# Masked row maxima of the two-block score tiles: memset and maximum in PSUM, or one VectorE instruction with an added mask

## The chip, the cores and the metric

One of the eight cores of a Trainium2 chip runs the kernel. The metric is the device time of one execution in microseconds (us), lower is better. The kernel before took 358.55 us, the median of 3 runs (357.07 to 360.89).

## The reference

For 8 batches and 8 heads, with 576 positions and 64 numbers per head, block-causal attention (blocks of 64 positions) is computed, and its output goes through a soft mixture of 8 experts with 4 slots each.

```
scores = q @ k.T / sqrt(64);  scores[block_i < block_j] = -1e9
attn = exp(scores - rowmax) / (rowsum + 1e-9);  x = attn @ v      # x: 4608 x 512
logits = x @ phi                                                   # 4608 x 32
slot inputs = softmax over positions of logits, transposed, @ x
h = relu(slot_input[e] @ w1[e]);  slot_out = h @ w2[e]
out = softmax over slots of logits @ slot_out
```

All inputs and the output are f32.

## The kernel before

The work goes by head pairs: 8 batches of 4 pairs make 32 pairs, numbered m. The 576 query rows of a head are handled in tiles that take only the keys a row may see. Tile "7" holds the 128 rows of blocks 6 and 7 with 512 keys, tile "5" the 128 rows of blocks 4 and 5 with 384 keys; each exists once for each of the two heads ("70", "71", "50", "51"). Tile "8" holds block 8 of both heads with 576 keys, and the tiles "3", "2", "1", "0" hold one block of both heads, with 256 to 64 keys. Only tiles 7 and 5 need a mask: their first 64 rows (partitions 0 to 63) may not see the last 64 keys.

For each pair the steps are these.

- SyncE (SP) loads q, k and v into slots of one large SBUF tile, `arena`, two slots each; POOL scales k (L420).
- PE forms the scores in PSUM: tile 7 and tile 5 in `qk` (L456), the others in `qkb` (L477). `scores` gives the PSUM bank of each; the table `BK` sets the banks.
- DVE takes the negated row maxima in `rowmax` into the small tile `stat`. Tile 7: a memset of 64x64 to -1e30 in PSUM (L492), then a TENSOR_REDUCE over 512 columns (L494). Tile 5: one memset of 64x128 for both heads (L488), then one TENSOR_REDUCE over both heads (768 columns, two results). The other tiles have a TENSOR_REDUCE alone, also L494.
- ACT takes the exponential in `expo` (L504): it reads the scores from PSUM, adds the negated maximum as bias, writes f32 probabilities into `arena` and the row sums into `stat`. In the trace that is an ACTIVATE and an ACTIVATION_READ_ACCUMULATOR.
- POOL adds epsilon to the sums (`zeps`, L514), DVE takes reciprocals (`zinv`, L510), POOL scales the probabilities (`norm`, L521).
- PE transposes the probabilities (L541), DVE and ACT copy them out of PSUM (L388 and L386), PE multiplies them with v (`pv`, L573, and `pv8`, L583), and the result is copied into `xT`.

Once a batch, the logits (L601, L608), the running softmax over positions and the slot inputs (L710, L730, L739, L748, L753) are added. From about 307 us on, the expert matmuls (L958, L978) and the output (L929 to L949) follow; nothing of the change runs there.

The order on each engine is written by hand: every step is recorded with a time by `at`, from the table `TM` (`rm70`, `rm71` and `rm5` are the maxima, one entry for both heads of tile 5), and the steps are issued in the order of those times. Each engine runs its own steps strictly in that order and waits on semaphores for the others. Eight matmuls on a zero tile, `idle`, run at the start (`warm`, L427); the tables that would place more of them (`FILL`, `FILL0`) are empty.

Of the kernel before, what the change touches and what calls it, by code (L numbers as in the profile page):

```python
# [10 lines left out]
BF16 = mybir.dt.bfloat16  # L11
AF = mybir.ActivationFunctionType
ALU = mybir.AluOpType
AX = mybir.AxisListType
# [9 lines left out]
EPS = 1e-9  # L24
NEG = -1e30


NC = {"7": 512, "5": 384, "8": 576, "3": 256, "2": 192, "1": 128, "0": 64}
# [3 lines left out]
COL = {"70": 0, "71": 1, "8": 2, "3": 3, "2": 4, "1": 5, "0": 6, "50": 7, "51": 8}  # L32
# [218 lines left out]
def tile_attention_softmoe(  # L251
# [9 lines left out]
    nc = tc.nc  # L261
    const = ctx.enter_context(tc.tile_pool(name="const", bufs=1))
# [11 lines left out]
            s0 = 16 * qd + 4 * g  # L274
            nc.vector.tensor_reduce(out=own[r, qd:qd + 1], in_=stack[r, s0:s0 + 4], axis=AX.X, op=ALU.add)

    idle = const.tile([128, 128], BF16, name="idle")
    nc.vector.memset(idle, 0.0)
    c_all = const.tile([128, 2, NC2, NS], F32, name="c_all")

# [52 lines left out]
    with ExitStack() as c1:  # L333
        xp = c1.enter_context(tc.tile_pool(name="xp", bufs=1, side="right"))
# [4 lines left out]
        def bank(k, i=0, z=""):  # L339
            n = BK.get(k + z, BK.get(k))[i]  # L340
            return ps_all[:, 512 * n:512 * n + 512]

        def banks(k, lo, n, z=""):
            a, c = BK.get(k + z, BK.get(k))
            return ps_all.rearrange("p (n c) -> p n c", c=512)[:, a:c + 1:c - a, lo:lo + n]
# [11 lines left out]
        phi_sb = area("phi").rearrange("p (c s) -> p c s", s=NS)  # L357

        dt = xp.tile([128, 256], F32, name="dt")

        def pads(late):
            if late:
                nc.gpsimd.memset(c_all, 0.0)
                return
            for x, n in (("8_0", 640), ("8_1", 640), ("2_0", 256), ("2_1", 256), ("0_0", 128), ("0_1", 128)):
                nc.gpsimd.memset(area("p" + x)[:, NC[x[0]]:n], 0.0)
            for i in range(NV):
                nc.gpsimd.memset(area(f"v{i}").rearrange("p (j c d) -> p j c d", j=2, c=NQ)[64:128, :, 4, :], 0.0)
            nc.gpsimd.memset(dt[:, 128:192], 0.0)
# [4 lines left out]
        def late(m):  # L374
            return {NP * NB - 1: "y", NP * NB - 2: "w", NP * NB - 3: "x", **FIRST}.get(m, f".{m % NP}")
# [19 lines left out]
        probs, xTs, xps = {}, {}, {}  # L395
# [28 lines left out]
        def warm(i):  # L424
            if i == 0:
                xps["w"] = bank("pb")
            nc.tensor.matmul(  # L427
                xps["w"], lhsT=idle[:, 0:128], rhs=idle[:, 0:64].unsqueeze(1).broadcast_to([128, 8, 64]), start=True, stop=True
            )


        def fill(bank, n):
            for _ in range(n):
                nc.tensor.matmul(
                    bank, lhsT=idle[:, 0:128], rhs=idle[:, 0:64].unsqueeze(1).broadcast_to([128, bank.shape[-1] // 64, 64]),
                    start=True, stop=True,
                )


        def scores(x, m):  # L440
            z = late(m)
            if x == "8":
                return banks("B8", 0, 288, z)
            if x[0] == "5":
                return bank("C5", int(x[1]), z)[:, 0:384]
            if x[0] == "7":
                return bank("A" + x, 0, z)
            j, lo = {"3": ("B30", 0), "0": ("B30", 256), "2": ("B21", 0), "1": ("B21", 192)}[x]
            return bank(j, 0, z)[:, lo:lo + NC[x]]
# [32 lines left out]

        def rowmax(m, x):
            st, u = stat[m % 2], COL[x if x != "5" else "50"]
            if x == "5":
                todo = [(u, 2, banks("C5", 0, 384, late(m)))]
                for _, n, sc in todo:
                    nc.vector.memset(sc[0:64, :, 320:384], NEG)  # L488
            else:
                todo = [(u, 1, scores(x, m))]  # L490
                if x[0] == "7":
                    nc.vector.memset(todo[0][2][0:64, 448:512], NEG)  # L492
            for u, n, sc in todo:
                nc.vector.tensor_reduce(  # L494
                    out=st[:, 0, u:u + n], in_=sc, axis=AX.XY if x == "8" else AX.X, op=ALU.max, negate=True
                )

        def expo(m, x):
            st, u = stat[m % 2], COL[x]
            sc = scores(x, m)  # L500
            pr = prob(m, x)[:, 0:NC[x[0]]]
            if x == "8":
                pr = pr.rearrange("p (n c) -> p n c", n=2)
            nc.scalar.activation(  # L504
                out=pr, in_=sc, func=AF.Exp, bias=st[:, 0, u:u + 1], accum_out=st[:, 1, u:u + 1],
            )

        def zinv(m, i):
# [3 lines left out]
        def zeps(m, i):  # L512
            st, c = stat[m % 2], slice(*ZG[i])
            nc.gpsimd.tensor_scalar(  # L514
                out=st[:, 2, c], in0=st[:, 1, c], scalar1=EPS, scalar2=1.0, op0=ALU.add, op1=ALU.mult
            )

        def norm(m, x):
# [276 lines left out]
        for i in range(WARM):  # L795
            at(-50 + 0.01 * i, warm, i)
# [32 lines left out]
        for k in AREAS:  # L829

            m = NM - 2 if k in ("q0", "ks0", "v0") or k[0] == "p" and k[-2:] == "_0" else NM - 1
            pvs = ("pv", "pa")
            ends[k] = end(m, ("UA", "UB", "UC") if k[0] in "qk" else pvs if k[0] == "v" or k[:2] == "pt" else GROUPS)
        for i in XIN:
            m = max(m for m in range(NM) if m % NXT == i)
# [19 lines left out]
    with ExitStack() as c2:  # L855
        start = c2.enter_context(ExitStack())
# [194 lines left out]
```

## Time and profile before

| what | before |
|---|---|
| median of 3 runs | 358.55 us (357.07 to 360.89) |
| the profiled execution | 360.34 us |
| its span, first to last instruction | 358.6 us |
| mean granted clock of TensorE | 0.988 |
| PE busy | 339.2 us, 95% of the span |
| DVE busy | 279.4 us, 78% |
| ACT busy | 258.3 us, 72% |
| POOL busy | 205.8 us, 57% |

PE is TensorE's matmuls, DVE VectorE, ACT ScalarE, POOL GpSimd, SP SyncE. L494 is line 494 of the kernel. Busy time is that of instructions; an engine that waits for another is not busy. The names in a row read output <- inputs: `ps` is PSUM, `arena` the large SBUF tile, `stat` the maxima, sums and reciprocals.

### The profile page before, as it was taken

The page shows a single profiled execution, that of the slowest core. Times are in us where ns is not written, and L with a number is a line of the kernel's source. Part 1 is how long each engine was busy: PE and PEld are TensorE (multiplying, and loading weights), DVE is VectorE, ACT ScalarE, POOL GpSimd, SP SyncE. Part 2 cuts the span into 40 slices and gives each one's busy share as a digit, 9 for nine tenths or more (in the row PEclk, how much of TensorE's full clock was granted, in tenths as well). Part 3 has the DMA queues.
Part 4 walks back from the last instruction along what each step waited for, and adds up shares of the span by engine and source line. Part 5 has one row for each costly group of instructions (what it writes and reads, how often), then busy time and mean ns, then how long its engine had stood idle before and what let it go on. Part 6 is the DMA issues. An engine that isn't in the chain of part 4 may idle for free.

```text
span 358.6 us, 14247 instructions
## 1 busy us (share of the span) xinstructions
PE 339.2 (95%) x5664; PEld 233.7 (65%) x5664; DVE 279.4 (78%) x750; ACT 258.3 (72%) x855; POOL 205.8 (57%) x475
## 2 busy tenths in 40 slices
PE   8899999998999999989999999999999999999990
PEld 3567677765777677757676777677766786337660
DVE  5989888995799979977999789978998856563351
ACT  3987888784898789868978897889788884122241
POOL 4786848854767676666757585758574872100000
PEclk9999999998999999999999999999999999999997
DMA  5676455375236744482268343841441139999987
GB/s 165 195 274 223 139 187 181 103 264 202 69 114 204 254 144 144 151 308 78 79 210 277 85 173 104 318 150 58 132 124 60 37 98 421 430 424 423 409 335 318
DMA packets 28929, 72.27 MB, mean 202 GB/s; under 512 B 6848, under 2 KB 15168, under 8 KB 23872
## 3 DMA queue, kind: packets, MB, share of 16 engines
q1 hardware_dynamic: 28864, 71.38, 56.2%
q8 instruction: 44, 0.72, 0.8%
q14 instruction: 21, 0.17, 0.1%
HBM read 61.93 MB, written 9.44 MB: 199 GB/s over the span
## 4 chain that ended last, share of the span: by engine, by line
PE 69%; DVE 9%; ACT 7%; POOL 5%; DMA 4%; issue 2%; SPq 0%; DVEq 0%; ACTq 0%; POOLq 0%
PE ps L541 14%; PE ps L573 13%; PE ps L456 12%; ACT arena L504 7%; DVE stat L494 6%; PE ps L477 6%; PE ps L583 5%; PE so L978 4%; PE hp L958 4%; POOL arena L521 3%; DMA arena<-in_v 3%; PE o L929 3%; PE ps L710 3%; PE ps L730 2%; PE ps L601 2%
## 5 line engine op out<-in xcount | busy, mean ns | idle before, releaser
L504 ACT ACTIVATE arena<-ps,stat 128x384 f32<-128x384 f32 (+6 forms) x288 | 153.2, 544 | 39.6 <-DVE stat L494 30.2
L521 POOL TENSOR_SCALAR arena<-arena,stat 128x384 f32<-128x384 f32 (+6 forms) x288 | 151.9, 544 | 32.1 <-DVE stat L510 18.6
L494 DVE TENSOR_REDUCE stat<-ps 128x1 f32<-128x512 f32 (+6 forms) x256 | 128.1, 543 | 4.2 <-ACT arena L504 0.2
L573 PE MATMUL ps<-arena 128*64 128x256 f32 (+2 forms) x640 | 77.0, 387 | 4.0 <-ACT arena L504 2.3
L388 DVE COPY arena<-ps 128x384 f32<-128x384 f32 (+3 forms) x136 | 70.0, 549 | 11.7 <-PE ps L541 5.0
L386 ACT COPY arena<-ps 128x384 f32<-128x384 f32 (+3 forms) x140 | 62.9, 518 | 10.5 <-PE ps L541 9.3
L541 PE MATMUL ps<-ident,arena 64*128 64x64 f32 x1600 | 67.4, 227 | 2.5 <-POOL arena L521 1.2
L541 PEld LDWEIGHTS ps<-ident,arena 64*128 64x128 f32 x1600 | 58.3, 139 | 13.4 <-POOL arena L521 5.8
L573 PEld LDWEIGHTS ps<-arena 128*64 128x64 f32 x640 | 42.0, 137 | 35.2 <-issue 18.8
L456 PE MATMUL ps<-arena 64*128 64x384 f32 (+1 forms) x256 | 59.0, 559 | 0.9 <-DMA arena<-in_q 0.5
L504 ACT ACTIVATION_READ_ACCUMULATOR arena<-ps,stat 128x1 f32 x288 | 59.8, 208 | 0.0
L514 POOL TENSOR_SCALAR stat<-stat 128x2 f32<-128x2 f32 (+1 forms) x96 | 18.7, 195 | 54.4 <-ACT arena L504 50.2
L477 PEld LDWEIGHTS ps<-arena 64*64 64x64 f32 x768 | 36.2, 132 | 21.1 <-ACT arena L386 9.1
L477 PE MATMUL ps<-arena 64*64 64x288 f32 (+4 forms) x768 | 42.9, 340 | 0.4 <-ACT arena L504 0.4
L456 PEld LDWEIGHTS ps<-arena 64*128 64x128 f32 x256 | 24.6, 188 | 15.9 <-DVE arena L388 4.5
L583 PE MATMUL ps<-arena 128*64 128x64 f32 x640 | 25.4, 227 | 0.4 <-DMA arena<-in_v 0.4
L583 PEld LDWEIGHTS ps<-arena 128*64 128x64 f32 x640 | 22.9, 140 | 1.4 <-ACT arena L504 0.5
L420 POOL TENSOR_SCALAR arena<-arena 128x576 f32<-128x576 f32 x32 | 21.5, 672 | 3.9 <-DMA arena<-in_k 3.0
L388 DVE COPY xn<-ps 128x512 f32<-128x512 f32 (+1 forms) x23 | 14.7, 649 | 10.8 <-PE ps L710 9.7
L939 DVE COPY arena<-o 128x512 f32<-128x512 f32 (+1 forms) x20 | 11.6, 632 | 11.9 <-PE o L929 11.9
L978 PEld LDWEIGHTS so<-arena,hT 128*32 128x32 f32 x512 | 13.5, 110 | 5.5 <-issue 5.1
L388 DVE COPY xT<-ps 128x512 f32<-128x512 f32 (+1 forms) x26 | 12.6, 502 | 4.9 <-PE ps L583 3.6
(113 smaller groups left out, 273.7 us busy)
## 6 DMA issues: line engine op xcount, KB each, us to landing
arena<-in_w SPq DMA_DIRECT2D x32, 1024.0 KB, 7.9
arena<-in_k SPq DMA_DIRECT2D x32, 288.0 KB, 3.3
arena<-in_q SPq DMA_DIRECT2D x32, 288.0 KB, 3.4
arena<-in_v SPq DMA_DIRECT2D x32, 256.0 KB, 4.1
out<-arena SPq DMA_DIRECT2D x7, 1024.0 KB, 5.3
out<-arena SPq DMA_DIRECT2D x4, 512.0 KB, 4.7
arena<-in_v SPq DMA_DIRECT2D x32, 32.0 KB, 3.8
arena<-in_phi SPq DMA_DIRECT2D x1, 64.0 KB, 2.6
```

The source lines that it names most:

```text
L386: nc.scalar.copy(out=out, in_=in_)
L388: nc.vector.tensor_copy(out=out, in_=in_)
L420: nc.gpsimd.tensor_scalar(out=area(f"ks{m % NQB}"), in0=area(f"ks{m % NQB}"), scalar1=SCALE, scalar2=0.0, op0=ALU.mult, op1=ALU.add)
L456: nc.tensor.matmul(scores(t + str(j), m), lhsT=q[r, lo:lo + 128], rhs=k[r, 0:NC[t]], start=True, stop=True)
L477: nc.tensor.matmul(o, lhsT=a, rhs=b, start=True, stop=True)
L494: nc.vector.tensor_reduce(out=st[:, 0, u:u + n], in_=sc, axis=AX.XY if x == "8" else AX.X, op=ALU.max, negate=True)
L504: nc.scalar.activation(out=pr, in_=sc, func=AF.Exp, bias=st[:, 0, u:u + 1], accum_out=st[:, 1, u:u + 1],)
L521: nc.gpsimd.tensor_scalar(out=pr, in0=pr, scalar1=st[:, 2, u:u + 1], scalar2=0.0, op0=ALU.mult, op1=ALU.add)
L541: nc.tensor.transpose(out=trbank(m, g)[i][:, 64 * n:64 * n + 64], in_=prob(m, x)[r, 128 * c:128 * c + 128], identity=ident[r, r],)
L573: nc.tensor.matmul(xps[m, 0][64 * j:64 * j + 64, lo:hi], lhsT=vs(m)[:, j, c, :], rhs=rhs, start=n == 0, stop=n == 4, skip_group_check=True,)
L583: nc.tensor.matmul(xps[m, 1][64 * j:64 * j + 64, 0:64], lhsT=vs(m)[:, j, c, :], rhs=arena[:, lo:lo + 64], start=(c == 0), stop=(c == NQ - 1),)
L978: nc.tensor.matmul(so[u][NS * g:NS * (g + 1), 0:CW], lhsT=hT[:, 4 * (n % 4) + g, :], rhs=pieces[i][:, 4 * (n % 4) + g, :], start=(n == 0), ...
```

## The change

The maxima of tiles 7 and 5 are taken by `tensor_tensor_reduce`. It reads the scores from PSUM and a bf16 mask from SBUF, adds the two, multiplies by -1, writes that back over the scores in PSUM, and keeps the minimum, which is the negated masked maximum. `expo` therefore reads these tiles with scale -1. The two heads of tile 5 are taken by two instructions in place of one. The mask is one tile of 320 columns, zero but for partitions 0 to 63 of its last 64 columns; an access pattern whose two halves overlap lays it over 512 or 384 columns. `idle` gives up 64 of its 128 columns, so the warm-up matmuls write 64 partitions in place of 128. `zeps` computes the sum times one plus epsilon, in place of the sum plus epsilon times one.

```diff
-    idle = const.tile([128, 128], BF16, name="idle")
+    idle = const.tile([128, 64], BF16, name="idle")
...
+        mask = xp.tile([128, 320], BF16, name="mask")
+        nc.vector.memset(mask, 0.0)
+        nc.vector.memset(mask[0:64, 256:320], NEG)
...
-                xps["w"], lhsT=idle[:, 0:128], rhs=idle[:, 0:64].unsqueeze(1).broadcast_to([128, 8, 64]), start=True, stop=True
+                xps["w"][0:64], lhsT=idle, rhs=idle[:, 0:64].unsqueeze(1).broadcast_to([128, 8, 64]), start=True, stop=True
...
         def rowmax(m, x):
             st, u = stat[m % 2], COL[x if x != "5" else "50"]
-            if x == "5":
-                todo = [(u, 2, banks("C5", 0, 384, late(m)))]
-                for _, n, sc in todo:
-                    nc.vector.memset(sc[0:64, :, 320:384], NEG)
+            if x in "75" or x[0] == "7":
+                for y in ("50", "51") if x == "5" else (x,):
+                    n = NC[y[0]] // 2
+                    sc = scores(y, m).rearrange("p (a n) -> p a n", a=2)
+                    ms = mask[:, 256 - n:256]
+                    ms = bass.AP(tensor=ms.tensor, offset=ms.offset, ap=[list(ms.ap[0]), [64, 2], [1, n]])
+                    nc.vector.tensor_tensor_reduce(
+                        out=sc, in0=sc, in1=ms, scale=-1.0, scalar=-NEG, op0=ALU.add, op1=ALU.min,
+                        accum_out=st[:, 0, COL[y]:COL[y] + 1],
+                    )
             else:
-                todo = [(u, 1, scores(x, m))]
-                if x[0] == "7":
-                    nc.vector.memset(todo[0][2][0:64, 448:512], NEG)
-            for u, n, sc in todo:
                 nc.vector.tensor_reduce(
-                    out=st[:, 0, u:u + n], in_=sc, axis=AX.XY if x == "8" else AX.X, op=ALU.max, negate=True
+                    out=st[:, 0, u:u + 1], in_=scores(x, m), axis=AX.XY if x == "8" else AX.X, op=ALU.max, negate=True
                 )
...
                 out=pr, in_=sc, func=AF.Exp, bias=st[:, 0, u:u + 1], accum_out=st[:, 1, u:u + 1],
+                scale=-1.0 if x[0] in "75" else 1.0,
...
-                out=st[:, 2, c], in0=st[:, 1, c], scalar1=EPS, scalar2=1.0, op0=ALU.add, op1=ALU.mult
+                out=st[:, 2, c], in0=st[:, 1, c], scalar1=1.0, scalar2=EPS, op0=ALU.mult, op1=ALU.add
```

On DVE, the maxima of the first pair of the fifth batch stand so before (these are the ones that ran at 174 us; `stat_108` is one of the two `stat` tiles, `ps` is PSUM):

```order
L510 RECIPROCAL stat_107<-stat_107 128x5
L492 MEMSET ps 64x64
L494 TENSOR_REDUCE stat_108<-ps 128x1
L488 MEMSET ps 64x2x64
L494 TENSOR_REDUCE stat_108<-ps 128x2
L492 MEMSET ps 64x64
L494 TENSOR_REDUCE stat_108<-ps 128x1 x6
L388 COPY xT_112<-ps 128x512
```

The same place on DVE with the change (ISA is the new instruction's name here: the first of two reads the scores and the mask, the second writes the accumulator out):

```order
L516 RECIPROCAL stat_107<-stat_107 128x5
L494 ISA ps,stat_108<-ps,mask 128x512
L494 ISA stat_108 128x1
L494 ISA ps,stat_108<-ps,mask 128x384
L494 ISA stat_108 128x1
L494 ISA ps,stat_108<-ps,mask 128x384
L494 ISA stat_108 128x1
L494 ISA ps,stat_108<-ps,mask 128x512
L494 ISA stat_108 128x1
L499 TENSOR_REDUCE stat_108<-ps 128x1 x5
L391 COPY xT_112<-ps 128x512
```

Six instructions (three memsets, three maxima) became eight; what stands ahead of them and behind them is what stood there, and no step changes its place on PE, ACT, POOL or SP.

At the start of DVE's list, before:

```order
L278 MEMSET idle 128x64
L289 MEMSET zrun 128x2
L298 MEMSET mrun_91 128x2
L291 MEMSET zrun 128x2
L267 COPY stack<-ident 128x32
```

and with the change:

```order
L278 MEMSET idle 128x32
L289 MEMSET zrun 128x2
L298 MEMSET mrun_91 128x2
L361 MEMSET mask 128x160
L362 MEMSET mask 64x64
L291 MEMSET zrun 128x2
```

The two memsets of the mask are new there.

## Rows read from the trace of the kernel before

**Rows 1.** Stretches: length; PE, PEld, DVE, ACT, POOL busy; granted clock; DMA share; GB/s.

```profile
0.00:25.00 25.00, 22.23 (x231) 12.97 (x233) 19.62 (x65) 17.50 (x60) 16.61 (x48) 1.00 0.62 206
25.00:287.00 262.00, 255.61 (x4309) 182.10 (x4307) 225.69 (x608) 214.86 (x729) 178.57 (x404) 0.99 0.48 158
205.00:241.00 36.00, 35.88 (x619) 25.37 (x611) 31.55 (x85) 30.17 (x104) 24.92 (x58) 1.00 0.54 186
84.00:86.00 2.00, 2.00 (x22) 1.45 (x20) 0.00 (x0) 0.45 (x2) 0.47 (x2) 0.50 0.95 374
```

**Rows 2.** Waits of PE between 25 and 287 us: us, times, longest.

```profile
PE ps L573 <- ACT arena L504: 2.3, 1, 2.3
PE ps L573 <- DMA arena<-in_v: 1.5, 1, 1.5
PE ps L541 <- POOL arena L521: 1.2, 6, 0.2
PE ps L583 <- DMA arena<-in_v: 0.4, 1, 0.4
PE ps L541 <- ACT arena L504: 0.3, 1, 0.3
```

**Rows 3.** Timeline of PE, the three places named below: start, duration, what.

```profile
82.25 3.30 PE L573 MATMUL ps<-arena 128*64 128x256 f32 x20 [2.33 <-ACT arena L504]
...
157.13 2.38 PE L573 MATMUL ps<-arena 128*64 128x256 f32 x20 [1.49 <-DMA arena<-in_v]
...
178.71 0.58 PE L541 MATMUL ps<-ident,arena 64*128 64x64 f32 x11 [0.34 <-ACT arena L504]
```

**Rows 4.** The chain of waits from 173 to 179 us: start, us, what.

```profile
174.02 0.12 DVE ps L492
...
174.88 0.18 DVE ps L488
...
175.08 0.96 DVE stat L494
...
176.41 2.26 ACT arena L504 x8
```

**Rows 5.** Groups of DVE instructions by form: busy us, mean ns, idle before.

```profile
L494 DVE TENSOR_REDUCE stat<-ps 128x1 f32<-128x512 f32 x64 | 44.3, 692 | 2.2
...
L494 DVE TENSOR_REDUCE stat<-ps 128x2 f32<-128x768 f32 x32 | 30.7, 959 | 1.1
...
L510 DVE RECIPROCAL stat<-stat 128x2 f32<-128x2 f32 x64 | 9.4, 154 | 0.1
...
L289 DVE MEMSET zrun<- 128x2 f32 x1 | 0.1, 60 | 0.0
```

**Rows 6.** Timeline of DVE, a two-source instruction and two copies behind it.

```profile
197.67 0.75 DVE L748 SCALAR_TENSOR_TENSOR acc<-acc,bm,ps 128x512 f32<-128x512 f32 x1 [0.38 <-ACT arena L504]
198.34 0.95 DVE L388 COPY arena<-ps 128x384 f32<-128x384 f32 x2
...
199.27 0.67 DVE L388 COPY arena<-ps 128x512 f32<-128x512 f32 x1
199.86 0.18 DVE L510 RECIPROCAL stat<-stat 128x5 f32<-128x5 f32 x1
```

**Rows 7.** Groups of ACT instructions by form, the accumulator read.

```profile
L504 ACT ACTIVATION_READ_ACCUMULATOR arena<-ps,stat 128x1 f32 x288 | 59.8, 208 | 0.0
```

**Rows 8.** Timeline of ACT at the start of the kernel.

```profile
7.22 0.58 ACT L504 ACTIVATE arena<-ps,stat 128x384 f32<-128x384 f32 x1 [4.99 <-PE ps L477]
```

**Rows 9.** Groups of POOL instructions by form.

```profile
L514 POOL TENSOR_SCALAR stat<-stat 128x2 f32<-128x2 f32 x64 | 12.2, 191 | 31.6 <-ACT arena L504 28.3
...
L514 POOL TENSOR_SCALAR stat<-stat 128x5 f32<-128x5 f32 x32 | 6.5, 203 | 22.9 <-ACT arena L504 21.9
```

**Rows 10.** Timeline of PE, the warm-up matmuls.

```profile
0.99 3.59 PE L427 MATMUL ps<-idle 128*128 128x512 bf16 x8 [0.99 <-DVE mrun L298]
```

More of the change, by code (lines that the diff above doesn't have):

```diff
@@ L434, in fill @@
                 nc.tensor.matmul(
-                    bank, lhsT=idle[:, 0:128], rhs=idle[:, 0:64].unsqueeze(1).broadcast_to([128, bank.shape[-1] // 64, 64]),
+                    bank[0:64], lhsT=idle, rhs=idle[:, 0:64].unsqueeze(1).broadcast_to([128, bank.shape[-1] // 64, 64]),
                     start=True, stop=True,
```

## The prediction

> **What bounds the kernel now.** I read first the table of stretches. From 25 to 287 us, where all the maxima but those of the first two pairs run, PE is busy 255.61 of 262 us and DVE 225.69; in 205 to 241 us, the length of one batch (four head pairs), PE is busy 35.88 of 36 us and DVE 31.55 [rows 1]. So PE is the bound, and DVE has about 4.4 us in each 36 that it does not use, 1.1 us per pair. Then PE's own waits in that stretch [rows 2]: 5.7 us in all, of which the rest to 6.4 is in pieces too small for the view. The largest, 2.3 us, is named after ACT; it stands before `pv` of a pair with the same form as the wait of 1.49 us at 157 us, which is named after the load of v [rows 3]. I take both as waits for v, and with the 0.4 us at L583 that makes 4.2 us of loads, which no maximum touches. What the maxima can reach is the remainder: 1.2 us in six waits of the transposes for POOL, and 0.3 us at 178.71 for ACT [rows 2, 3].
>
> Then the chain [rows 4]. It leaves PE and runs through DVE in 174.02 to 176.04 us (the memset and maximum of one tile 7, then memset and maximum of tile 5), then through four exponentials on ACT, and comes back to PE at the wait of 178.71. Much of the DVE share of the chain is of this kind, but PE has other work meanwhile, so that taking 0.5 us off the DVE part gives PE only the wait it had.
>
> **The change part by part: DVE's time.** Before, one pair costs by starts: memset and maximum of tile 7 take 0.86 us from memset to memset (174.02 to 174.88), and of tile 5, 0.20 us from memset to maximum and 0.96 us for the maximum [rows 4]. With two tiles 7 that is 2 x 0.86 + 1.16 = 2.88 us.
>
> With the change a pair has two new instructions of 512 columns, two of 384, and four accumulator reads. No row shows the new instruction. The nearest is SCALAR_TENSOR_TENSOR, which also reads one operand from PSUM and one from SBUF: 0.75 us long, and its follower starts 0.67 us after it [rows 6]. For 384 columns I take off 128 times 1.04 ns, the slope between the maxima of 512 and 768 columns (692 and 959 ns) [rows 5]: 0.67 - 0.13 = 0.54 us. The accumulator read writes one number per partition; a memset of two columns took 60 ns and a reciprocal of two columns 154 ns [rows 5], and I take 0.10 us. Sum: 2 x (0.67 + 0.10) + 2 x (0.54 + 0.10) = 2.82 us, against 2.88: nothing, 0.06 us per pair.
>
> The bounds. Cheapest: the new instruction runs as a plain copy from PSUM, 0.59 us from start to start (199.27 to 199.86) [rows 6], 0.46 us for 384 columns, and the read costs 0.06 us: 2 x 0.65 + 2 x 0.52 = 2.34 us, 0.54 us per pair less. Dearest at full rate: no overlap with its follower, 0.75 and 0.62 us, and a read of 0.20 us as on ACT, where it has a mean of 208 ns [rows 7]: 2 x 0.95 + 2 x 0.82 = 3.54 us, 0.66 us per pair more.
>
> The Trainium skill (VectorE: DVE Perf Modes, Rules for kernel authors) says that fusing DVE operations buys nothing as such and that the count of instructions is to be kept low; here the count rises from six to eight per pair. Its Vector Engine (DVE) Microarchitecture Reference (Measured stream behaviour on trn2) gives 1.0417 ns per column and about 75 ns per instruction; an estimate by that page is 2048 columns and six instructions before, 2.58 us, and 1796 columns and eight instructions after, 2.47 us. By it DVE would gain 0.11 us per pair where I have 0.06; the rows of before are 0.30 us above it, part of which is the semaphore between memset and maximum.
>
> **The change part by part: when the exponentials may start.** For tile 7, the maximum was ready 0.86 us after the first DVE instruction and is now ready at about 0.77 us. For tile 5, both heads were ready after 1.16 us; now the first is ready at 0.64 us and the second at 1.28 us. ACT takes one head after the other, so its start moves 0.52 us ahead, and the second head, 0.12 us later than before, comes while ACT is still at the first. This is the gain, and it is counted where ACT waits on it and PE behind ACT. At the start, ACT's first exponential is one of tile 5 and starts at 7.22 us after a wait [rows 8]; I take 0.4 us there, since ACT is then the engine that runs without a break. At 178.71 the wait of 0.3 us goes. Of the six waits for POOL, whose epsilon step sits behind ACT, I count four of 0.2 us: 0.8 us at most, and take 0.5, because DVE's reciprocal stands between. Sum: 0.4 + 0.3 + 0.5 = 1.2 us. What is late next is PE itself, in its order.
>
> **The small edits, together.** Scale -1 on ACT changes no count and no size: nothing. Epsilon: POOL's step takes 191 ns for two numbers and 203 ns for five [rows 9], and is mostly fixed cost; the other order of multiply and add can be worth 20 ns either way, 96 times, on an engine that sat idle 54 us before these very steps: nothing, covered by the wait for ACT, at most 0.3 us where POOL is waited for. The mask's two memsets fill DVE's idle time before 2.27 us: nothing. The warm-up matmuls stream 512 columns each as before, eight in 3.59 us [rows 10], some 0.43 us apart, which is the lower of TensorE's levels (512 columns at 1.2 GHz); with 64 output partitions they should run as long. If the engine came to 2.4 GHz later than before, the first scores would be slower; PE waits in that stretch anyway (busy 22.23 of 25 us [rows 1]). I take nothing, with bounds of -0.3 and +1.5 us.
>
> The sum against the profiled execution: 360.34 (span 358.6, and 1.7 around it) - 1.2 = 359.1 us. That execution lies 1.8 us above the median of the runs, so against the median 358.55 the forecast is 357.4 us. A measurement of this kernel can tell about 1% (3.6 us) from no change, so this is no change that can be told.
>
> **Rivals.** First, PE hides everything. For it: PE's 35.88 of 36 us [rows 1]. Against it: ACT's wait at 178.71 does reach PE. Time: 358.5 us.
>
> Second, slower by the accumulator read. The place is the four reads per pair on DVE; each is an instruction between the new one and the next of the hand-written order. At the dear bound DVE gets 0.66 us more per pair, 2.6 of the 4.4 us that it has free in a batch. DVE also copies the transposed probabilities out of PSUM, and PE needs those banks; PE has 0.12 us of slack in that batch. If a quarter of the 32 x 0.66 = 21 us shows on PE, the time is 358.5 + 5.3, near 363.8 us. It decides from about 0.3 us per pair on, since below that the earlier start of tile 5 pays for it. For it: the read on ACT costs 208 ns [rows 7]. Against it: DVE's own small instructions take 60 to 154 ns [rows 5].
>
> Third, slower by a halved rate. The place is the main new instruction: two operands, a result in the same PSUM bank as the first operand, and an accumulator. At two cycles per column 512 columns take 1.20 us and 384 take 0.94; with the reads 4.68 us per pair, 1.8 us more, 7.2 per batch where 4.4 are free. DVE would then be the bound with 38.8 us per batch in place of 36, and over 262 us that is 20 us: 378.5 us. It decides as soon as DVE's extra time passes 1.1 us per pair. Against it: SCALAR_TENSOR_TENSOR with an operand of each memory runs near one column per cycle (0.67 us for 512 [rows 6]). The Trainium skill (Vector Engine (DVE) Microarchitecture Reference, Points that are easy to get wrong) says that instructions of the SCALAR_TENSOR_TENSOR kind with two sources in SBUF, neither of them bf16, run at half rate because both read ports are taken and none is left for the accumulator. Here one source is in PSUM and the mask is bf16, so by its wording the rule doesn't hold, and the row above, without an accumulator, neither confirms nor excludes it.
>
> Fourth, faster by over 1%. DVE at the cheap bound (0.54 us per pair less), all of the 1.5 us of waits behind ACT and POOL gone, 0.8 us at the start, and with everything earlier one of the two waits for v as well: 2.3 us, and what came behind it. After that wait the granted clock fell to 0.50, the lower level, in 84 to 86 us [rows 1], and `pv` took 3.30 us where it takes 2.38 [rows 3], 0.9 us more. Sum 1.5 + 0.8 + 2.3 + 0.9 = 5.5 us: 353 us. For it: ACT waits on the maxima before many tiles. Against it: the loads of v hang on their own queue, not on DVE.
>
> **How the numbers follow.** The forecast (357.4 us) 0.37, PE hides everything 0.22, the dear read 0.17, the halved rate 0.06, faster 0.18. So faster by over 1% 0.18, within 1% 0.59, slower by over 1% 0.23. The range goes from 353.5, just inside the fast rival, to 364.5 us, just beyond the dear read; the halved rate and the ends are left out.
>
> **What would show it.** Right: the new instruction near 0.75 us for 512 columns and 0.61 for 384 in DVE's groups; accumulator reads of 60 to 150 ns; DVE busy per batch within 0.5 us of 31.55; ACT's exponentials of tile 5 waiting some 0.5 us less in total per pair; no wait of PE at the place of 178.71. Wrong: the new instruction at 1.1 us or more (third rival); reads at 200 ns and PE waiting on copies by DVE (second); waits for v gone and a span under 354 us (fourth).

## The result and the profile after

The changed kernel takes 354.42 us (median of 4 runs, 353.48 to 355.47), the kernel before, in runs beside it, 358.94 us (median of 4, 357.07 to 360.89). The ratio is 0.988, with an interval of 0.983 to 0.992: 4.5 us faster. Run again on another occasion (e5 below) the same change gave 0.983 (0.978 to 0.989). All ratios in this text are to the kernel before, run beside, and of fast runs alone, those within 1.5% of a kernel's fastest; in e5 that leaves 4 of 12 runs, and the medians of all runs there give 0.995 (356.60 against 358.47 us). The forecast was 357.4 us with a range from 353.5 to 364.5: the time is inside, at the fast end, and the sign of the sum was right, but the 1.2 us of the sum were about a quarter of what came. The lower end of the range was taken from the fourth rival (353 us), so that the time lies inside it owes nothing to the sum.

The profiled execution of the changed kernel took 353.48 us, its span 351.4 us, at a mean granted clock of 0.992. Its page begins so; the columns are busy time, share of the span and instructions of each engine:

```profile
PE 333.5 (95%) x5664; PEld 231.7 (66%) x5664; DVE 269.8 (77%) x816; ACT 258.0 (73%) x855; POOL 205.9 (59%) x475
```

PE is as busy as before by share (95%, in a span 7.2 us shorter), DVE 9.6 us less busy, and ACT and POOL the same. The groups of DVE and POOL instructions by form, which answer to [rows 5] and [rows 9]:

```profile
L494 DVE CUSTOM_DVE_ANT_1 ps<-ps,mask 128x512 f32<-128x512 f32 x64 | 44.1, 713 | 5.3 <-PE ps L459 4.0 <-ACT arena L389 0.2
...
L494 DVE CUSTOM_DVE_ANT_1 ps<-ps,mask 128x384 f32<-128x384 f32 x64 | 34.9, 585 | 1.2 <-PE ps L459 1.1
...
L494 DVE DVE_READ_ACCUMULATOR2_ANT stat<- 128x1 f32 x128 | 18.0, 141 | 0.0
L520 POOL TENSOR_SCALAR stat<-stat 128x2 f32<-128x2 f32 x64 | 12.3, 191 | 25.3 <-ACT arena L509 22.2
L520 POOL TENSOR_SCALAR stat<-stat 128x5 f32<-128x5 f32 x32 | 6.6, 207 | 23.2 <-ACT arena L509 22.3
```

The new instruction is 713 and 585 ns long (forecast: 0.75 and 0.61 us), the accumulator read 141 ns (forecast: 60 to 150), the epsilon step as long as before within 4 ns. Lengths are not what a queue pays, though. The timeline of DVE at the place that [rows 4] show before, the first pair of the fifth batch:

```profile
167.32 0.70 DVE L494 CUSTOM_DVE_ANT_1 ps<-ps,mask 128x512 f32<-128x512 f32 x1
167.93 0.14 DVE L494 DVE_READ_ACCUMULATOR2_ANT stat<- 128x1 f32 x1
167.96 0.57 DVE L494 CUSTOM_DVE_ANT_1 ps<-ps,mask 128x384 f32<-128x384 f32 x1
168.45 0.14 DVE L494 DVE_READ_ACCUMULATOR2_ANT stat<- 128x1 f32 x1
168.45 0.60 DVE L494 CUSTOM_DVE_ANT_1 ps<-ps,mask 128x384 f32<-128x384 f32 x1
168.97 0.14 DVE L494 DVE_READ_ACCUMULATOR2_ANT stat<- 128x1 f32 x1
168.97 0.73 DVE L494 CUSTOM_DVE_ANT_1 ps<-ps,mask 128x512 f32<-128x512 f32 x1
169.61 0.14 DVE L494 DVE_READ_ACCUMULATOR2_ANT stat<- 128x1 f32 x1
169.61 1.83 DVE L499 TENSOR_REDUCE stat<-ps 128x1 f32<-128x128 f32 x5
```

Read the starts. The accumulator read and the next instruction start together (168.45, 168.97, 169.61), or 0.03 us apart (167.93 and 167.96): the read costs DVE's queue nothing here. From 167.32 to 169.61 one pair takes 2.29 us. Before, the pair at this place began at 174.02 [rows 4], and its last maximum of 512 columns, with no memset behind it, began at 176.19, as the timeline of DVE before shows:

```profile
176.04 0.11 DVE L492 MEMSET ps<- 64x64 f32 x1
176.19 0.89 DVE L494 TENSOR_REDUCE stat<-ps 128x1 f32<-128x512 f32 x2
```

A reduction of 512 columns with no memset behind it gives way after some 0.6 us (0.61 by a row of e2 below, 0.59 by one of e9), so the pair took 2.17 + 0.6 = 2.77 us. The prediction had 2.88, since it counted a memset behind each maximum. So the change takes 0.48 us off DVE's queue per pair, 15.4 us over 32 pairs, of which 4.5 us reach the end.

Where did the time come out of? The waits of PE, from 25 to 280 us, do not tell it:

```profile
PE ps L579 <- DMA arena<-in_v: 2.6, 2, 1.8
PE ps L589 <- DMA arena<-in_v: 1.7, 1, 1.7
PE ps L547 <- POOL arena L527: 0.9, 3, 0.4
```

The waits for v are 4.3 us where they were 4.2 [rows 2]; they moved to other pairs. The transposes wait 0.9 us for POOL where they waited 1.2, and the 0.3 us for ACT are gone. That is 0.6 us of 4.5. The rest is in instructions that look busy. The group of the transposes, before and after:

```profile
L541 PE MATMUL ps<-ident,arena 64*128 64x64 f32 x1600 | 67.4, 227 | 2.5 <-POOL arena L521 1.2 <-ACT arena L504 0.8
```

```profile
L547 PE MATMUL ps<-ident,arena 64*128 64x64 f32 x1600 | 64.9, 227 | 1.7 <-POOL arena L527 0.9 <-ACT arena L509 0.2
```

The same 1600 transposes of 227 ns are busy 2.5 us less. A transpose's record is 227 ns long, but they start far closer together than that (a run of 50 can be over in 1.79 us, as at 161.24 below), so a gap of up to some 0.19 us between two of them is covered by the first one's record. One place, which comes again in other batches, shows it, 19.5 us behind the first logits matmul at 130.90 us before and 19.4 us behind the one at 125.52 us after. Timelines before, of PE, then of PEld (the weight loads), then of POOL:

```profile
150.45 2.38 PE L541 MATMUL ps<-ident,arena 64*128 64x64 f32 x50
152.67 0.65 PE L456 MATMUL ps<-arena 64*128 64x512 f32 x2
...
161.24 1.79 PE L541 MATMUL ps<-ident,arena 64*128 64x64 f32 x50
...
150.45 0.85 PEld L541 LDWEIGHTS ps<-ident,arena 64*128 64x128 f32 x18
151.46 1.24 PEld L541 LDWEIGHTS ps<-ident,arena 64*128 64x128 f32 x32 [0.15 <-POOL arena L521]
...
150.33 2.46 POOL L521 TENSOR_SCALAR arena<-arena,stat 128x192 f32<-128x192 f32 x5
```

The same place after:

```profile
144.93 1.95 PE L547 MATMUL ps<-ident,arena 64*128 64x64 f32 x50
146.69 1.75 PE L459 MATMUL ps<-arena 64*128 64x512 f32 x8
...
144.93 1.82 PEld L547 LDWEIGHTS ps<-ident,arena 64*128 64x128 f32 x50
...
144.11 2.46 POOL L527 TENSOR_SCALAR arena<-arena,stat 128x192 f32<-128x192 f32 x5
```

Before, POOL starts to scale the probabilities 0.12 us ahead of the transposes that read them, after 0.82 us ahead. The 50 transposes give way to the scores of the next pair after 2.22 us before (150.45 to 152.67) and 1.76 us after. PE has no idle time in either row; only PEld shows a piece of the wait. A gain of 0.46 us in one place, and none of it in the waits of PE. Two batches on it is the same: the rows begin at 224.10 us before and 216.87 after, and the scores 2.22 and 1.76 us behind.

By batches, from the first logits matmul of one to that of the next, in those in the middle of the kernel without a wait for v: 35.96, 36.23 and 36.09 us before (from 94.94, 168.17 and 204.40 us), 35.69 and 35.76 us after (from 89.83 and 161.51). The second of these after, in the columns of [rows 1]:

```profile
161.51:197.27 35.76, 35.48 (x614) 25.31 (x612) 30.47 (x93) 30.18 (x103) 25.01 (x57) 1.00 0.49 161
```

DVE is busy 30.47 us of 35.76, where it was 31.55 of 36 [rows 1]. The means differ by 0.37 us; taken for seven batches, an estimate, that is 2.6 us. The first batch gives more: its first logits matmul came at 52.46 us before and 52.19 after, although a wait for v took 1.75 us after and 0.37 before, so 1.65 us of it was saved elsewhere. Together some 4.2 us, about what the medians differ by (4.5). The two profiled executions lie further apart, 6.9 us; part of that is the lower clock level of the one before behind its wait at 82 us [rows 1, 3], which the one after does not have.

### The profile page after: what moved, and what is told of

Read it like the earlier page. It is cut to its first block, busy times and chain, and to the rows that moved or that the text cites. A ratio compares the mean times of both kernels' runs of the same rounds, so it can differ in the third digit from the quotient of the medians.

```text
span 351.4 us, 14291 instructions
## 1 busy us (share of the span) xinstructions
PE 333.5 (95%) x5664; PEld 231.7 (66%) x5664; DVE 269.8 (77%) x816; ACT 258.0 (73%) x855; POOL 205.9 (59%) x475
## 4 chain that ended last, share of the span: by engine, by line
PE 76%; DMA 7%; DVE 5%; POOL 5%; ACT 3%; issue 2%; SPq 1%; DVEq 0%; POOLq 0%
PE ps L579 16%; PE ps L547 14%; PE ps L459 12%; PE ps L480 8%; DMA arena<-in_v 6%; PE ps L589 5%; PE so L984 4%; PE hp L964 4%; POOL arena L527 4%; PE ps L716 3%; ACT arena L509 3%; PE o L935 3%; PE ps L607 2%; DVE ps L494 2%; PE ps L736 2%
## 5 line engine op out<-in xcount | busy, mean ns | idle before, releaser
L509 ACT ACTIVATE arena<-ps,stat 128x384 f32<-128x384 f32 (+6 forms) x288 | 152.7, 543 | 30.5 <-DVE stat L494 23.6
L494 DVE CUSTOM_DVE_ANT_1 ps<-ps,mask 128x512 f32<-128x512 f32 (+1 forms) x128 | 76.5, 649 | 6.4 <-PE ps L459 5.1
L579 PE MATMUL ps<-arena 128*64 128x256 f32 (+2 forms) x640 | 76.1, 384 | 2.7 <-DMA arena<-in_v 2.6
L547 PE MATMUL ps<-ident,arena 64*128 64x64 f32 x1600 | 64.9, 227 | 1.7 <-POOL arena L527 0.9
L547 PEld LDWEIGHTS ps<-ident,arena 64*128 64x128 f32 x1600 | 57.0, 139 | 11.2 <-POOL arena L527 2.9
L579 PEld LDWEIGHTS ps<-arena 128*64 128x64 f32 x640 | 41.7, 137 | 32.9 <-issue 18.3
L499 DVE TENSOR_REDUCE stat<-ps 128x1 f32<-128x128 f32 (+4 forms) x160 | 56.3, 401 | 3.4 <-PE ps L480 2.7
L520 POOL TENSOR_SCALAR stat<-stat 128x2 f32<-128x2 f32 (+1 forms) x96 | 18.9, 197 | 48.5 <-ACT arena L509 44.5
L589 PEld LDWEIGHTS ps<-arena 128*64 128x64 f32 x640 | 22.3, 138 | 2.8 <-ACT arena L509 1.9
L494 DVE DVE_READ_ACCUMULATOR2_ANT stat<- 128x1 f32 x128 | 18.0, 141 | 0.0
```

Of the source, the lines that this page charges most:

```text
L494: nc.vector.tensor_tensor_reduce(out=sc, in0=sc, in1=ms, scale=-1.0, scalar=-NEG, op0=ALU.add, op1=ALU.min, accum_out=st[:, 0, COL[y]:COL[ ...
L499: nc.vector.tensor_reduce(out=st[:, 0, u:u + 1], in_=scores(x, m), axis=AX.XY if x == "8" else AX.X, op=ALU.max, negate=True)
L509: nc.scalar.activation(out=pr, in_=sc, func=AF.Exp, bias=st[:, 0, u:u + 1], accum_out=st[:, 1, u:u + 1], scale=-1.0 if x[0] in "75" else 1.0,)
L547: nc.tensor.transpose(out=trbank(m, g)[i][:, 64 * n:64 * n + 64], in_=prob(m, x)[r, 128 * c:128 * c + 128], identity=ident[r, r],)
L579: nc.tensor.matmul(xps[m, 0][64 * j:64 * j + 64, lo:hi], lhsT=vs(m)[:, j, c, :], rhs=rhs, start=n == 0, stop=n == 4, skip_group_check=True,)
L589: nc.tensor.matmul(xps[m, 1][64 * j:64 * j + 64, 0:64], lhsT=vs(m)[:, j, c, :], rhs=arena[:, lo:lo + 64], start=(c == 0), stop=(c == NQ - 1),)
```

## The experiments

The theories that the expectations name: D, VectorE's time per head pair counts, wherever it lies; E, the earlier first head of tile 5 is what counts (the prediction's own term); S, the small edits (idle tile with its warm-up, epsilon) count. They were written with 0.59 us per pair for the change; by the recount above it is 0.48.

**e1, tile 7 alone.** The new instruction for tile 7; tile 5 keeps its memset and its one maximum over both heads.

```diff
-            if x in "75" or x[0] == "7":
-                for y in ("50", "51") if x == "5" else (x,):
+            if x[0] == "7":
+                for y in (x,):
...
+            elif x == "5":
+                sc = banks("C5", 0, 384, late(m))
+                nc.vector.memset(sc[0:64, :, 320:384], NEG)
+                nc.vector.tensor_reduce(out=st[:, 0, u:u + 2], in_=sc, axis=AX.X, op=ALU.max, negate=True)
...
-                scale=-1.0 if x[0] in "75" else 1.0,
+                scale=-1.0 if x[0] == "7" else 1.0,
```

> The new instruction on tile 7 alone; tile 5 keeps its memset and its one maximum over both heads. By starts, DVE's masked maxima of a pair would take 2 x 0.63 + 1.16 = 2.42 us, against 2.88 before and 2.28 with the whole change. Theory D (DVE's shorter time per pair is what PE gains from, through everything that DVE does): most of the gain, 0.46 of 0.60 us per pair, so some 3.5 us of the 4.5: about 355.5. Theory E (the gain is that the first head of tile 5 is ready earlier): little or nothing, 358 to 359. Theory S (the small edits, warm-up and epsilon): the full gain, 354.5.

Measured: ratio 0.993 (0.988 to 0.998), 2.5 us, a little less than D had (3.5). One pair of its DVE takes 2.46 us by starts, 0.31 less than before.

**e2, tile 5 alone.** The other half: tile 7 keeps memset and maximum.

```diff
-            if x in "75" or x[0] == "7":
-                for y in ("50", "51") if x == "5" else (x,):
+            if x == "5":
+                for y in ("50", "51"):
...
+                if x[0] == "7":
+                    nc.vector.memset(scores(x, m)[0:64, 448:512], NEG)
...
-                scale=-1.0 if x[0] in "75" else 1.0,
+                scale=-1.0 if x[0] == "5" else 1.0,
```

> The new instruction on tile 5 alone; tile 7 keeps memset and maximum. DVE's masked maxima of a pair: 1.72 + 1.03 = 2.75 us against 2.88, and the first head of tile 5 is ready some 0.5 us earlier. Theory D: 0.13 of 0.60 us per pair, about 1 us: 358. Theory E: the full gain, 354.5 to 355. Theory S: 354.5.

Measured: ratio 0.997 (0.992 to 1.002), so no gain that can be told. Its timeline of DVE:

```profile
171.64 0.11 DVE L500 MEMSET ps<- 64x64 f32 x1 [0.19 <-PE ps L459]
171.78 0.69 DVE L501 TENSOR_REDUCE stat<-ps 128x1 f32<-128x512 f32 x1
172.39 0.56 DVE L494 CUSTOM_DVE_ANT_1 ps<-ps,mask 128x384 f32<-128x384 f32 x1
172.86 0.14 DVE L494 DVE_READ_ACCUMULATOR2_ANT stat<- 128x1 f32 x1
172.86 0.60 DVE L494 CUSTOM_DVE_ANT_1 ps<-ps,mask 128x384 f32<-128x384 f32 x1
173.38 0.14 DVE L494 DVE_READ_ACCUMULATOR2_ANT stat<- 128x1 f32 x1
173.52 0.11 DVE L500 MEMSET ps<- 64x64 f32 x1
```

From 171.64 to 173.52 it is 1.88 us, and memset and maximum of the second tile 7 make it 2.63: 0.14 us less than before. The read at 173.38 costs 0.14 us here, where a memset follows it. This half starts the first head of tile 5 early, as the whole change does, and gains hardly anything: against E.

**e3, the small edits alone** on the kernel before.

```diff
-    idle = const.tile([128, 128], BF16, name="idle")
+    idle = const.tile([128, 64], BF16, name="idle")
...
-                out=st[:, 2, c], in0=st[:, 1, c], scalar1=EPS, scalar2=1.0, op0=ALU.add, op1=ALU.mult
+                out=st[:, 2, c], in0=st[:, 1, c], scalar1=1.0, scalar2=EPS, op0=ALU.mult, op1=ALU.add
```

> The kernel before with the narrower warm-up tile and the other order of epsilon alone. Theories D and E: no change, 358.5 to 359.2. Theory S: 354.5.

Measured: ratio 1.003 (0.999 to 1.006). S falls. The set-up of the mask is not in this kernel; it is in e4 and e12, where the gain is gone all the same.

**e4, the time given back to DVE.** The changed kernel with one more reduction of 512 columns on constants behind tile 5's maxima, 0.60 us by starts.

```diff
+        dump = xp.tile([128, 1], F32, name="dump")
...
+                if x == "5":
+                    nc.vector.tensor_reduce(
+                        out=dump, in_=ident.unsqueeze(1).broadcast_to([128, 4, 128]), axis=AX.XY, op=ALU.max, negate=True
+                    )
```

> The whole change, and per pair one more maximum on DVE over 512 columns of an SBUF tile, into a number that nobody reads, right behind the maxima of tile 5: 0.61 us per pair, which gives back what the change took off DVE. Theory D: back to the time before, 358 to 360. Theory E: the first head of tile 5 is as early as with the change, so the time stays near 354.5 to 355.5.

Measured: ratio 1.000 (0.996 to 1.004). Everything of the change is still in this kernel but DVE's time, and the gain is gone. The added reduction reads SBUF alone, so DVE's time counts also where it does not touch PSUM.

**e5, the changed kernel again,** without an edit, as a measure beside e6 to e8.

> The changed kernel once more, as the base on the chip of this group. All theories: ratio to before 0.983 to 0.992, about 354.5.

Measured: ratio 0.983 (0.978 to 0.989), overlapping with the first measurement, 0.988 (0.983 to 0.992).

**e6, the heads of tile 5 swapped.** DVE takes head 1 first, while ACT still takes head 0 first, so ACT's start on tile 5 comes one instruction later.

```diff
-                for y in ("50", "51") if x == "5" else (x,):
+                for y in ("51", "50") if x == "5" else (x,):
```

> The changed kernel with the two heads of tile 5 taken in the other order on DVE (51, then 50), while ACT still asks for 50 first: the first exponential of tile 5 now waits for both, 1.03 us in place of 0.52 us behind the first DVE instruction, and DVE's time is the same. Theory D: as the changed kernel, within 0.7 us. Theory E: the gain is lost, 357.5 to 359.

Measured: ratio 0.990 (0.985 to 0.994). Without the earlier start most or all of the gain is there. D wanted it within 0.7 us of the changed kernel: it lies 0.4 us above the first measurement (354.84 against 354.42), and its interval overlaps with e5's, whose middle is 2.3 us lower.

**e7, two maxima for tile 5** on the kernel before: the memset stays, then one maximum of 384 columns for each head. Its first head is ready early, at no less time on DVE (2.83 us per pair).

```diff
-                todo = [(u, 2, banks("C5", 0, 384, late(m)))]
-                for _, n, sc in todo:
-                    nc.vector.memset(sc[0:64, :, 320:384], NEG)
+                nc.vector.memset(banks("C5", 0, 384, late(m))[0:64, :, 320:384], NEG)
+                todo = [(COL[y], 1, scores(y, m)) for y in ("50", "51")]
```

> The kernel before, but tile 5 in one memset and two maxima, one per head. DVE's time stays (0.20 + 2 x 0.47 = 1.14 us against 1.16), the first head is ready about 0.4 us earlier. Theory D: no change, 358 to 359. Theory E: most of the gain, 355 to 356.

Measured: ratio 1.002 (0.999 to 1.005). The earlier start by itself is worth nothing that shows; E falls.

**e8, no mask.** The kernel before without the memsets of tiles 7 and 5, so their mask is left out and the maxima alone are taken, 2.15 us per pair.

```diff
-                for _, n, sc in todo:
-                    nc.vector.memset(sc[0:64, :, 320:384], NEG)
...
-                if x[0] == "7":
-                    nc.vector.memset(todo[0][2][0:64, 448:512], NEG)
```

> The kernel before without the memsets of PSUM: the mask of tiles 7 and 5 is left out, the maxima stay as they were. DVE's masked maxima of a pair take 2 x 0.61 + 0.88 = 2.10 us by starts, 0.78 us less than before and 0.18 less than with the change; no head of tile 5 is ready early (0.96 us against 1.16). Theory D: at or a little below the changed kernel, 353 to 354.5. Theory E: 357.5 to 358.5.

Measured: ratio 0.984 (0.979 to 0.990). With 0.14 us per pair less on DVE than the changed kernel, its time can't be told from that kernel's (0.988 and 0.983). Plain maxima without any new instruction give the same gain, so it is the queue's time and not a property of the instruction.

**e9, more time on DVE in the kernel before:** the reduction of e4, behind tile 5's maximum.

```diff
+        dump = xp.tile([128, 1], F32, name="dump")
...
+            if x == "5":
+                nc.vector.tensor_reduce(
+                    out=dump, in_=ident.unsqueeze(1).broadcast_to([128, 4, 128]), axis=AX.XY, op=ALU.max, negate=True
+                )
```

> The kernel before, with one more VectorE reduction of 512 columns (on constants, its result unused) behind the maxima of tile 5 of every head pair: +0.6 us of VectorE per pair, 32 pairs, 19.5 us in all; nothing else differs. Theory D (VectorE's time per pair counts, by about a quarter: the change took 0.59 us x 32 = 18.9 us off VectorE and 4.5 us came out): a quarter of 19.5 us, about 363 us, ratio 1.010 to 1.017. Rival C, the ceiling of the prediction read both ways (TensorE is the bound and covers VectorE on either side): under 1 us, ratio under 1.003. Rival W (VectorE is the bound in this stretch): most of 19.5 us, ratio over 1.035.

Measured: ratio 1.023 (1.017 to 1.028), 8.1 us (6.2 to 9.9) for 32 times 0.59 us. More than the quarter of D, less than the bound of W, and far from C. Its timeline of DVE:

```profile
189.28 0.96 DVE L495 TENSOR_REDUCE stat<-ps 128x2 f32<-128x768 f32 x1
190.16 0.68 DVE L499 TENSOR_REDUCE dump<-ident 128x1 f32<-128x512 f32 x1
190.75 1.21 DVE L495 TENSOR_REDUCE stat<-ps 128x1 f32<-128x192 f32 x3
```

The added reduction is 0.68 us long and gives way after 0.59 (190.16 to 190.75): the figure used above for a maximum of 512 columns.

**e10, more time on PE in the kernel before,** and **e11, the same in the changed kernel:** one matmul of 512 bf16 columns on zeros ahead of the transposes of group gd of each pair.

```diff
         def tr(m, g):
+            if g == "gd":
+                fill(trbank(m, g)[0], 1)
```

> The kernel before, with one more matmul of 512 bf16 columns on zeros ahead of the transposes of group gd of every head pair (the transposes write its bank anew): about 0.21 us of TensorE per pair, 6.8 us in all. Rival C (TensorE is the bound, its stream has no hidden waits): all of it, about 365 us, ratio 1.017 to 1.021. Theory D (TensorE waits in pieces too short for its record to show): these waits take up a good part of it, ratio 1.003 to 1.012.

> The changed kernel with the same added matmul. With VectorE's time gone from its way, TensorE is nearer to being the bound: theory D expects a larger share of the 6.8 us here than in the kernel before, ratio to the kernel before 0.995 to 1.005. Rival C expects all of it in both, so the distance between the two stays the 4.5 us of the change: ratio 1.005 to 1.009.

Measured: e10 1.018 (1.014 to 1.021), e11 1.005 (1.003 to 1.008). As the expectations stand, e10 lies where C wanted it and outside D's range, and e11 at the edge of both. But their price of 0.21 us was too low. The timeline of PE in e10:

```profile
177.78 2.38 PE L575 MATMUL ps<-arena 128*64 128x256 f32 x20
180.09 0.39 PE L434 MATMUL ps<-idle 128*128 128x512 bf16 x1
180.41 0.76 PE L543 MATMUL ps<-ident,arena 64*128 64x64 f32 x12
181.10 0.80 PE L585 MATMUL ps<-arena 128*64 128x64 f32 x20
```

The added matmul takes 0.32 us from start to start, not 0.21; over all 32 pairs of e10 it is 0.31 to 0.32, so 10.2 us in all. At that price C stands for 1.028, outside e10's interval: 6.3 us (4.9 to 7.6) showed. This place is the one of 178.71 before [rows 3]. From the start of `pv` to that of `pv8` it takes 3.32 us here, with the added matmul (177.78 to 181.10), and 3.43 us in the kernel before, without it (175.79 to 179.22): it stands wholly inside the wait. In the group of the transposes of e10 the busy time falls as well:

```profile
L543 PE MATMUL ps<-ident,arena 64*128 64x64 f32 x1600 | 63.9, 227 | 0.6 <-ACT arena L504 0.3 <-POOL arena L521 0.2
```

67.4 us before, 63.9 here, for the same 1600 transposes, and their idle time falls from 2.5 to 0.6. So at least 3.5 us of what the kernel before shows as busy transposes was waiting, and the added work took it up. At 0.32 us C wants 10.2 us in both kernels, D less, and a larger part of it in the changed one. Shown are 6.3 us in e10 and 6.3 us in e11 (1.005 against 0.988; 7.8 us against 0.983). C falls by e10, with a price measured after the expectation was written, and by e9; that more shows in the changed kernel is neither shown nor excluded.

**e12, the reduction at another place:** the changed kernel with e4's reduction behind the copy of the pair's output.

```diff
+        dump = xp.tile([128, 1], F32, name="dump")
...
             copy("xa" if lo else "xb", xTs[m][:, lo:hi], xps.pop((m, int(lo > 0)))[:, 0:hi - lo], late(m))
+            if lo == 0:
+                nc.vector.tensor_reduce(
+                    out=dump, in_=ident.unsqueeze(1).broadcast_to([128, 4, 128]), axis=AX.XY, op=ALU.max, negate=True
+                )
```

> The changed kernel with the added VectorE reduction of the earlier run (512 columns, +0.6 us per pair) at another place: behind the copy of the head pair's output instead of behind the maxima of tile 5. Theory D as it stands (VectorE's time per pair counts, wherever it lies): the same loss as there, ratio about 1.000 to the kernel before. Rival P (only what lies between the scores and the exponentials counts, elsewhere VectorE has waits that take it up): the gain stays, ratio 0.984 to 0.991.

Measured: ratio 1.004 (1.001 to 1.007). The gain is gone here as well, so P falls: it is not only the stretch from the scores to the exponentials that counts.

Put in order of DVE's time per pair against the kernel before, by starts. The last column is the group of the 1600 transposes in the one profiled execution of each: busy time and the idle time of PE just before them, in us.

| kernel | us per pair | ratio | transposes |
|---|---|---|---|
| e8, no mask | -0.62 | 0.984 | 64.5 + 2.0 |
| the change (twice) | -0.48 | 0.988, 0.983 | 64.9 + 1.7, 64.8 + 2.1 |
| e6, heads swapped | -0.43 | 0.990 | 64.6 + 2.1 |
| e1, tile 7 alone | -0.31 | 0.993 | 66.9 + 1.4 |
| e2, tile 5 alone | -0.14 | 0.997 | 65.7 + 2.0 |
| before | 0 | 1 | 67.4 + 2.5 |
| e7, two maxima | +0.06 | 1.002 | 66.9 + 4.8 |
| e12, given back elsewhere | +0.11 | 1.004 | 67.6 + 4.2 |
| e4, given back | +0.12 | 1.000 | 67.0 + 3.2 |
| e9, more than before | +0.59 | 1.023 | 67.7 + 10.0 |

The ratios follow DVE's time: 0.29 of each microsecond taken off DVE comes out (4.5 of 15.4; 0.18 to 0.39 by the interval), and 0.43 of each one added (8.1 of 18.9; 0.33 to 0.52). The transposes follow it too: the sum of the last column is 3.3 us less with the change than before, of the 4.5 us, and 7.8 us more in e9, of its 8.1. So most of what DVE's time is worth shows where PE transposes the probabilities. No kernel tried is faster than the change by more than the intervals.

## Why the prediction was right in its range and small in its sum

**DVE's time.** The term "nothing, 0.06 us per pair" was mis-sized. Before, a pair takes 2.77 us and not 2.88; after, 2.29 and not 2.82. The new instruction gives way after 0.61 to 0.64 us for 512 columns and 0.49 to 0.52 for 384 in the pair shown, where 0.67 and 0.54 were taken, and the accumulator read, taken at 0.10 us, costs 0. The result lies just under the cheap bound of 2.34 us, whose read at 0.06 us was still too dear. DVE's 30.47 us per batch lie 1.08 us under 31.55, outside the 0.5 us that were named as a sign of being right.

The Trainium skill (VectorE: DVE Perf Modes, Rules for kernel authors) advises to keep the number of DVE operations low and not to fuse for speed. Here the number rose from six to eight per pair and the time fell, because the four reads hide beside the instruction behind them, and three memsets with the gaps behind them went. The half rate that the Trainium skill (Vector Engine (DVE) Microarchitecture Reference, Points that are easy to get wrong) gives for instructions of the SCALAR_TENSOR_TENSOR kind with two sources in SBUF, neither of them bf16, did not come up with one source in PSUM and a bf16 mask: 0.61 us for 512 columns is about 1.2 ns per column with all fixed cost in it. No run here puts both sources into SBUF.

**The ceiling.** The other step that failed is "What the maxima can reach is the remainder: 1.2 us ... and 0.3 us", and with it "PE is the bound", drawn from 35.88 busy of 36 us. PE's busy share hides waits shorter than a record. e10 shows 3.5 us of them in the transposes alone, and the transposes' group gave back 2.5 us with the change. A price of one quarter for time that DVE gets more was in the text, in the second rival; the same quarter on time that DVE gets less would have been near what the runs gave (0.29), and the ceiling forbade it. Both steps were needed for the small sum: a quarter of its own 0.06 us per pair would have been 0.5 us. The Trainium skill (Perfetto Trace Analysis, Identifying the Most-Contended Engine) says that the busy share of matmuls is no good measure of how near a kernel is to TensorE's roofline, and to take the share of peak arithmetic and the busy share of weight loads in its place. This trace agrees: PE is 95% busy in both kernels, weight loads 65% before and 66% after, and the time still fell.

**When the exponentials may start.** Of the 1.2 us, the wait for ACT at 178.71 went (0.3 us), but six transposes on in the same run PE now waits 0.26 us for POOL. The place before, from `pv` to `pv8`, and after:

```profile
175.79 2.38 PE L573 MATMUL ps<-arena 128*64 128x256 f32 x20
...
179.22 0.80 PE L583 MATMUL ps<-arena 128*64 128x64 f32 x20
```

```profile
169.13 2.38 PE L579 MATMUL ps<-arena 128*64 128x256 f32 x20
171.44 0.40 PE L547 MATMUL ps<-ident,arena 64*128 64x64 f32 x6
172.10 0.40 PE L547 MATMUL ps<-ident,arena 64*128 64x64 f32 x6 [0.26 <-POOL arena L527]
172.43 0.80 PE L589 MATMUL ps<-arena 128*64 128x64 f32 x20
```

It takes 3.43 us before and 3.30 after, so 0.13 us came of it and not 0.3, and the sign "no wait of PE at the place of 178.71" did not come. All waits of the transposes for POOL, this one among them, fell by 0.3 us, not 0.5. At the start ACT's first exponential begins so:

```profile
6.26 0.58 ACT L509 ACTIVATE arena<-ps,stat 128x384 f32<-128x384 f32 x1 [4.03 <-DVE stat L494]
```

Before it began at 7.22 [rows 8]: 0.96 us earlier, where 0.4 was taken; 0.2 to 0.3 us of that is PE's, whose scores of tile 5 began at 4.64 us for 4.84 and those of the next tiles at 5.48 for 5.77. The reason given, the earlier first head of tile 5, falls with e6 and e7: the gain comes with the queue's time, wherever it is saved (e12), not with that start. ACT's exponentials wait 23.6 us on the new maxima and 3.6 us on the others,

```profile
ACT arena L509 <- DVE stat L494: 23.6, 33, 4.0
ACT arena L509 <- DVE stat L499: 3.6, 6, 0.7
```

and before they waited 30.2 us on all, and 1.5 us more that the profile puts down to DVE's memsets: 4.5 us less, some 0.14 us per pair, not 0.5.

**The small edits.** Nothing, as said: e3 gives 1.003 with 1 inside its interval, and the warm-up matmuls end no later (eight in 3.51 us from 0.95, before 3.59 from 0.99 [rows 10]). The prediction took the lower clock level from their distance of some 0.43 us; the granted clock is 1.00 in that stretch [rows 1], so no row shows that level as granted there.

**The rivals.** That PE hides everything is excluded by the result and, from the other side, by e9. The dear read is excluded by the timeline (0 in place of 0.20 us), the halved rate by the starts. The fourth, faster, had the right half: DVE at the cheap bound. The time is nearer to it (353 us) than to the forecast (357.4). Its other half, one wait for v and the clock behind it, is not what the runs show: waits for v are 4.3 us after the change. And runs with a mean granted clock of 0.994 or 0.995 beside each other differ as well: e6 took 353.67, 354.48 and 354.84 us, the kernel before 358.47 in the median of 11. It also bounded the waits behind ACT and POOL by 1.5 us, the same ceiling.

**What stays open.** Which of DVE's steps PE waits for: the maxima (by ACT, POOL's scaling and the transposes, as the pair at 145 us shows) or also the copies out of PSUM. e4 and e12 lose the gain at both places, and nothing tried tells the two paths apart. In e9 the profile puts 4.3 of the 10.0 us of idle time before the transposes down to ACT and 2.0 to DVE's copies into `xT`, in e12 1.3 of the 4.2 to DVE's copies into `arena`, so both may play a part. Whether more shows of time added to DVE than of time taken off is open too: the two intervals overlap, and the second measurement of the change gives 0.40.

## What to carry to other kernels

A busy share of 95% on PE, or of 35.88 us in 36, is no ceiling for what another engine's time can give: where short matmuls or transposes overlap in the trace, waits up to a record's length look like work. Look at the same run of instructions in different pairs (1.79, 1.95, 2.38 us for 50 transposes) and at the waits of the weight loads. Price a microsecond on the second engine the same way in both directions; here 0.3 to 0.4 of it shows. And price an instruction by the distance to the start of the next, in the order in which it will stand, not by its length.

## What was not expected of the hardware

An accumulator read of 141 ns costs its queue nothing when another streaming instruction follows (both start at 168.45), and 0.14 us when a memset follows (173.38 to 173.52 in e2). The instruction with scores from PSUM, a bf16 mask from SBUF, a result written over the scores and an accumulator gives way as fast as a plain maximum of the same width: 0.61 to 0.64 us for 512 columns, against 0.61 (171.78 to 172.39 in e2). And a single matmul of 512 bf16 columns between f32 work takes 0.32 us from start to start in e10, at a granted clock of 1.00 from 25 to 350 us.
